# Batch 0 of an attention and SwiGLU kernel: v through the loading queue of q and k, cast on the compute engines

## The chip, the cores and the metric

The kernel runs on one core of one Trainium2 chip. The metric is the device time of one execution in microseconds (us). The kernel before takes 317.82 us, the median of three runs (317.57 to 317.85). One further execution was recorded by the hardware profiler: it took 317.75 us, and the span from its first to its last recorded instruction is 316.0 us. All times inside the kernel below count from the start of that span.

A core has five instruction streams that run side by side and meet at semaphores. TensorE (PE) multiplies matrices, and its weight loads are listed apart as PEld. VectorE (DVE) and ScalarE (ACT) work on elements, GpSimd (POOL) casts and issues DMAs, SyncE (SP) issues DMAs. Each stream executes its instructions strictly in the order in which the program holds them. Sixteen DMA engines move the data that the queues of SP, POOL and ACT ask for.

## The reference

```python
q_s = np.exp(q - np.max(q, axis=-1, keepdims=True))
q_s = q_s / (np.sum(q_s, axis=-1, keepdims=True) + 1e-09)
k_s = np.exp(k - np.max(k, axis=2, keepdims=True))
k_s = k_s / (np.sum(k_s, axis=2, keepdims=True) + 1e-09)
kv = np.einsum('bhsd,bhse->bhde', k_s, v)
attn = np.einsum('bhsd,bhde->bhse', q_s, kv)        # batch 8, heads 8, 576 tokens, head size 64
x = attn.transpose(0, 2, 1, 3).reshape(4608, 512)
g = x @ w_gate                                      # 512 x 1536
out = (g / (1 + np.exp(-g)) * (x @ w_val)) @ w_out  # 1536 x 512
```

This is linear attention: q is normalized over the head dimension, k over the tokens, and the 64x64 product of k and v per head is applied to q. Its output, 4608 tokens of 512 channels, goes through a SwiGLU block. All inputs and the output are float32.

## The kernel before

**Layout.** A batch has 8 heads, handled as two groups G of 4 heads. A loaded tile of q, k or v has 128 partitions: two heads g in the upper and lower half, 64 token blocks each, and along the free axis two heads h and 576 values (9 tokens t of 64). `head_ap` (L65) describes that access to memory, and `load` (L72) issues it on SP into one of three rotating buffers per tensor. A load is 576 KB in float32, in rows of 2304 bytes.

**Attention.** For each group, ScalarE takes the exponent of q and k into bf16 (`exp_of`, L119). VectorE sums q over the head dimension, takes the reciprocal and multiplies (`norm_sum`, `norm_mul`). For batch 0 TensorE transposes the normalized q (`turn_pe`) and a copy moves the result out of PSUM (`turn_out`). `key_sum` (L393) sums the keys by matmuls against the selector `sel`. `kv_first` (L404) multiplies keys by v in 18 matmuls, `scale_first` (L417) divides by the key sums, `x_mm` (L213) applies the result to the transposed q, and `x_out` (L228) copies it to `xt`, which holds x transposed: 4 blocks of 128 channels, blocks 0 and 1 from group 0, blocks 2 and 3 from group 1.

**SwiGLU.** `m_unit` (L286) computes one block m of 128 of the 1536 hidden channels for a chunk of tokens. It contracts `xt` with `wg` into gate banks and with `wv` into value banks, over the 4 channel blocks kk. For 576 tokens it has two parts, of 320 and 256. ScalarE applies Silu, VectorE multiplies into `hr`. `o_mm` (L318) contracts `hr` with `wo`. Twelve units for batch 0 come first, then batch 1's attention among output matmuls, and then eight chunks whose units have the attention of later batches between them.

**What sets the order.** The program is written under a manual schedule: each engine gets its instructions in the order of the source text. Around the change there are these queues:

- SP issues q and k of group 0, then q and k of group 1. The loads of batch 1 follow, and the first of them waits until the second slice of `wo` has landed (L454, `w_dma[-3]`).
- POOL issues v of batch 0 with a cast to bf16 during the transfer (L358 to L361), directly into the constant tiles `v16`; the first of these waits until k of group 0 has landed. Behind them stand the weights, also cast in transfer, in slices of 256, 384, 384 and 512 columns of `wg` and `wv` (L380), then four slices of `wo`. POOL allows eight of its DMAs in flight.
- The text from L426 to L452 sets the order on PE, ACT and DVE: warm-up matmuls (`spin`), key sums, transposes, the kv products, and the copies to `xt`.

In the first unit of batch 0 (`by_part=True`) the steps are sorted by part: gate and value of the first 320 tokens, then of the other 256. [...]

Of the kernel before, what the change touches and what calls it, by code (L numbers as in the profile page):

```python
# [11 lines left out]
SYNC = mybir.DependencyInfo(mybir.DependencyClass.Sync, mybir.DependencyReason.DATA)  # L12
# [3 lines left out]
def kernel(  # L16
# [10 lines left out]
    nc = tc.nc  # L27
# [6 lines left out]
    T = S // 64  # L34
# [27 lines left out]

    raw = {}

    def head_ap(src, b, G, t0=0, t1=T):  # L65
        return bass.AP(
            tensor=src.tensor,
            offset=src[b, 4 * G].offset + 64 * t0,
            ap=[[T * 64, 128], [2 * HSTR, 2], [1, (t1 - t0) * 64]],
        )  # L70

    def load(what, src, b, G, pieces=((0, T),), after=None):  # L72
        t_ = ld.tile([128, 2, T * 64], FP32, tag=what, name=what)
        raw[what, b, G] = t_
        last = None
        for t0, t1 in pieces:
            last = nc.sync.dma_start(out=t_[:, :, 64 * t0:64 * t1], in_=head_ap(src, b, G, t0, t1))
# [54 lines left out]
    def norm_sum(b, G, pieces=((0, T),)):  # L132
        s = st[b, G]
        eq2 = s["eq"].rearrange("p t h d -> p (t h) d")
        rs = at.tile([128, 2 * T], FP32, tag="rs", name="rs")
        first = None
        for t0, t1 in pieces:
            i = nc.vector.reduce_sum(  # L138
                out=rs[:, 2 * t0:2 * t1], in_=eq2[:, 2 * t0:2 * t1, :], axis=mybir.AxisListType.X
            )  # L140
            first = first or i
        rr = s["rr"] = at.tile([128, 2 * T], FP32, tag="rr", name="rr")
        nc.vector.reciprocal(out=rr, in_=rs)
        return first

    def norm_mul(b, G, pieces=((0, T),), engs=None):
# [3 lines left out]
        for (t0, t1), eng in zip(pieces, engs or (nc.vector, nc.vector)):  # L150
            n = 2 * (t1 - t0)
            eng.tensor_mul(  # L152
                qs[:, t0:t1, :].rearrange("p t (h d) -> p (t h) d", d=64),
                eq2[:, 2 * t0:2 * t1, :],
                s["rr"][:, 2 * t0:2 * t1].to_broadcast([128, n, 64]),
            )

    def turn_pe(b, G, i):
        s = st[b, G]
        if i == 0:  # L160
            s["qt"] = at.tile([128, T, 128], BF16, tag="qt", name="qt")
        t0, t1 = BANKS[i]
        tp = s["tp", i] = psp.tile([128, 1024], BF16, tag="ps", name="tp")
        for t in range(t0, t1):
            j = t - t0
            nc.tensor.transpose(  # L166
                out=tp[:, j * 128:(j + 1) * 128], in_=s["qs"][:, t, :], identity=ident
            )
# [15 lines left out]
    def ek_of(b, G, g, t):  # L184
        return st[b, G]["ek"][64 * g:64 * g + 64, t, :, :].rearrange("p h d -> p (h d)")
# [49 lines left out]
    def x_one(b, G):  # L235
        for i in range(2):
            x_out(b, G, i, x_mm(b, G, i))
# [45 lines left out]

    def m_unit(c0, n, m, by_part=False):  # L286
        ms = slice(m * 128, (m + 1) * 128)
        parts = [(c0, n)] if n <= 512 else [(c0, 320), (c0 + 320, n - 320)]
        gu = []
        for nm in ("g_ps", "u_ps"):  # L290
            ps = [bank(nm) for _ in parts]
            gu.append(ps)
        steps = [(a, kk, i) for a in range(2) for kk in range(KT) for i in range(len(parts))]
        if by_part:
            steps.sort(key=lambda a: (a[2], a[0], a[1]))
        for a, kk, i in steps:
            c, w_ = parts[i]
            nc.tensor.matmul(  # L298
                out=gu[a][i][:, 0:w_], lhsT=(wg, wv)[a][:, kk, ms], rhs=xt[:, kk, c:c + w_],
                start=(kk == 0), stop=(kk == KT - 1),  # L300
            )
# [49 lines left out]

    make_identity(nc, ident)
    with tc.manual_schedule():
        kd = []
        for G in range(NG):
            load("q", q, 0, G)
            kd.append(load("k", k, 0, G))
        d = nc.gpsimd.dma_start(out=v16[0], in_=head_ap(v, 0, 0))  # L358
        tc.add_manual_dep(d.ins, kd[0].ins.name, SYNC, reason="order of loads")
        for t0, t1 in BANKS:  # L360
            nc.gpsimd.dma_start(out=v16[1][:, :, 64 * t0:64 * t1], in_=head_ap(v, 0, 1, t0, t1))  # L361

        warm = const.tile([128, 1], FP32, name="warm", tag="warm")
        nc.vector.memset(warm, 0.0)
# [11 lines left out]
        first = norm_sum(0, 0, BANKS)  # L376
        norm_mul(0, 0, BANKS)
        norm_sum(0, 1, BANKS)

        for c0, n in ((0, 256), (256, 384), (640, 384), (1024, 512)):  # L380
            w_slice(wg, moe_w_gate, c0, n)
            w_slice(wv, moe_w_val, c0, n)
        w_dma = [wo_slice(m0, 3) for m0 in (0, 3, 6, 9)]

        def spin(n, after=None):
            idle = bank("idle")
            for _ in range(n):
# [16 lines left out]
        def kv_first(G, t0=0, t1=T):  # L404
            s = st[0, G]
            if t0 == 0:
                s["kv"] = [bank("kv") for _ in range(2)]
            for t in range(t0, t1):
                for g in range(2):
                    r = slice(64 * g, 64 * g + 64)  # L410
                    nc.tensor.matmul(
                        out=s["kv"][g][:, 0:128].rearrange("p (h d) -> p h d", d=64),
                        lhsT=ek_of(0, G, g, t), rhs=v16[G][r, :, 64 * t:64 * t + 64],
                        start=(t == 0), stop=(t == T - 1),
                    )

        def scale_first(G, eng1):  # L417
# [3 lines left out]
            if eng1 is nc.scalar:  # L421
                nc.scalar.mul(kn[:, 1, :], s["kv"][1][:, 0:128], s["kvr"][:, 1:2])
            else:
                nc.vector.tensor_scalar_mul(kn[:, 1, :], s["kv"][1][:, 0:128], s["kvr"][:, 1:2])
# [21 lines left out]
        x_out(0, 0, 0, xp0[0], (nc.scalar, nc.scalar))  # L446
        x_out(0, 0, 1, xp0[1], (nc.vector, None))
        scale_first(1, nc.vector)
        xp1 = x_mm(0, 1, 0), x_mm(0, 1, 1)
        x_out(0, 1, 0, xp1[0], (nc.scalar, nc.vector))  # L450
        x_out(0, 0, 1, xp0[1], (None, nc.vector))
        x_out(0, 1, 1, xp1[1], (nc.scalar, nc.vector))  # L452

        load_batch(1, w_dma[-3], by_group=True)  # L454
        load_batch(2)

        for m in range(MT):
            m_unit(0, S, m, by_part=(m == 0))

        exp_of("q", 1, 0)  # L460
        exp_of("k", 1, 0)
# [121 lines left out]
```

The softmax here doesn't subtract the row's maximum and nothing guards it: scores larger than these inputs give would overflow.

## Time and profile before

| What | Value |
|---|---|
| Median of three runs | 317.82 us |
| Profiled span | 316.0 us |
| PE busy | 304.7 us, 96% |
| DVE busy | 163.2 us, 52% |
| ACT busy | 147.6 us, 47% |
| POOL busy | 28.0 us, 9% |
| SP's queue (q1) | 39.99 MB |
| POOL's queue (q0) | 5.31 MB, counted as written in bf16 |

A table of windows gives, for each stretch of time, its length and then the busy time and the number of instructions of PE, PEld, DVE, ACT and POOL, the granted clock of PE, the share of DMA time and GB/s. A timeline line gives start and duration in us, the engine, the source line, the operation, what it writes from what with its shape, and in brackets how long the engine had been idle before it and what ended the idle time. A line with x2 is two instructions merged. In the rows of DMA queues the columns are packets, MB and the packet time as a share of 16 engines. An idle engine costs time only where it is on the chain that ends last.

### The profile page before, as it was taken

Reading aid. Unit: us, or ns where it says so; the run is one execution under the profiler, and the core shown is the slowest. Engines: PE = TensorE matmul, PEld = TensorE weight load, DVE = VectorE, ACT = ScalarE, POOL = GpSimd, SP = SyncE. Lnnn points to the kernel's source line nnn. Section 1 sums busy time; section 2 is a strip of 40 time slices with the busy share of each in tenths; the row PEclk is TensorE's granted clock in tenths of the full one; section 3 lists DMA queues with packets and bytes.
Section 4 is the critical chain, followed back from the end, with each engine's and each line's share of the span. In section 5 each row is a group of like instructions: output and inputs, shape, how many; then the busy total and the mean of one; then the engine's idle time right before and its main releaser. Section 6 shows DMA issues by size and latency. Waiting matters only on the chain.

```text
span 316.0 us, 4856 instructions
## 1 busy us (share of the span) xinstructions
PE 304.7 (96%) x1865; PEld 152.0 (48%) x1894; DVE 163.2 (52%) x277; ACT 147.6 (47%) x218; POOL 28.0 (9%) x35
## 2 busy tenths in 40 slices
PE   6799999999999999999999999999999999999994
PEld 2477744554444444544454444544454444444443
DVE  3834476685754566455835492639354333423421
ACT  4743488634663465447354637355743113312300
POOL 2930021100200020002000200020000000000000
PEclk9999999999999999999999999999999999999999
DMA  7999999269246806490629253944310202020124
GB/s 269 183 204 207 296 393 391 68 160 364 50 91 179 338 17 128 112 394 11 141 68 352 97 110 66 322 162 103 66 41 0 65 3 66 0 68 3 31 68 102
DMA packets 39304, 45.75 MB, mean 145 GB/s; under 512 B 16368, under 2 KB 23024, under 8 KB 39280
## 3 DMA queue, kind: packets, MB, share of 16 engines
q1 hardware_dynamic: 32480, 39.99, 42.0%
q0 software_dynamic: 6640, 5.31, 10.9%
q8 instruction: 15, 0.25, 0.3%
q10 hardware_dynamic: 160, 0.13, 0.2%
q14 instruction: 9, 0.07, 0.1%
HBM read 37.75 MB, written 9.44 MB: 149 GB/s over the span
## 4 chain that ended last, share of the span: by engine, by line
PE 88%; DMA 4%; DVE 3%; ACT 2%; issue 1%; POOL 1%; SPq 0%; DVEq 0%
PE g_ps L298 29%; PE u_ps L298 29%; PE o_ps L322 25%; PE kv L191 3%; DMA wv<-in_moe_w_val_dram 2%; DMA k<-in_k_dram 2%; DVE rs L138 1%; PE xp L267 1%; DVE qs L152 1%; PE o_ps L342 1%; ACT L124 1%; ACT eq L124 1%; POOL v L361 0%; PE tp L166 0%; POOL v L358 0%
## 5 line engine op out<-in xcount | busy, mean ns | idle before, releaser
L305 ACT ACTIVATE sg<-g_ps 128x512 bf16<-128x512 f32 (+2 forms) x120 | 65.1, 554 | 139.1 <-PE g_ps L298 120.7
L306 DVE TENSOR_TENSOR hr<-sg,u_ps 128x512 bf16<-128x512 bf16 (+2 forms) x120 | 74.5, 630 | 87.8 <-PE u_ps L298 80.4
L298 PE MATMUL g_ps<-xt,wg 128*128 128x512 bf16 (+2 forms) x469 | 110.0, 358 | 1.0 <-ACT xt L111 0.2
L298 PE MATMUL u_ps<-xt,wv 128*128 128x512 bf16 (+2 forms) x468 | 109.8, 357 | 1.2 <-DMA wv<-in_moe_w_val_dram 0.5
L322 PE MATMUL o_ps<-wo,hr 128*128 128x512 bf16 x414 | 93.0, 379 | 0.4 <-issue 0.2
L298 PEld LDWEIGHTS <-wv 128*128 128x128 bf16 x480 | 46.9, 98 | 47.2 <-DMA wv<-in_moe_w_val_dram 0.9
L298 PEld LDWEIGHTS <-wg 128*128 128x128 bf16 x480 | 45.8, 98 | 45.3 <-issue 0.7
L322 PEld LDWEIGHTS <-hr 128*128 128x128 bf16 x420 | 40.9, 98 | 49.1
L113 DVE COPY o_sb<-o_ps 128x512 f32<-128x512 f32 x33 | 22.4, 680 | 39.2 <-PE o_ps L322 37.3
L127 POOL CAST vb<-v 128x1152 bf16<-128x1152 f32 x14 | 16.0, 1146 | 174.3 <-DMA v<-in_v_dram 111.8
L138 DVE TENSOR_REDUCE rs<-eq 128x18 f32<-128x1152 bf16 (+2 forms) x18 | 21.7, 1214 | 13.2 <-ACT eq L124 13.2
L152 DVE TENSOR_TENSOR qs<-eq,rr 128x1152 bf16<-128x1152 bf16 (+2 forms) x18 | 22.1, 1237 | 0.1
L124 ACT ACTIVATE eq<-q 128x1152 bf16<-128x1152 f32 (+2 forms) x18 | 18.1, 1050 | 4.5 <-DMA q<-in_q_dram 4.4
L124 ACT ACTIVATE ek<-k 128x1152 bf16<-128x1152 f32 x16 | 18.0, 1158 | 0.3 <-DMA k<-in_k_dram 0.2
L305 ACT ACT_TABLE_LOAD x12 | 15.4, 1283 | 0.2
L124 ACT ACT_TABLE_LOAD x11 | 14.1, 1283 | 0.2
L388 PE MATMUL idle<-zero 128*128 128x512 bf16 x20 | 6.1, 459 | 3.0 <-DVE rs L138 1.8
L191 PE MATMUL kv<-vb,ek 64*128 64x129 bf16 x252 | 8.7, 217 | 0.0
L191 PEld LDWEIGHTS <-ek 64*128 64x128 bf16 x252 | 7.3, 94 | 2.7 <-ACT sg L305 2.1
L275 ACT CAST xt<-xp 128x512 bf16<-128x512 f32 x12 | 6.4, 588 | 3.6 <-PE xp L267 3.6
L276 DVE CAST xt<-xp 128x512 bf16<-128x512 f32 x12 | 7.7, 683 | 0.0
L347 ACT COPY o_sb<-o_ps 128x128 f32<-128x128 f32 x2 | 0.5, 265 | 13.3 <-DVE o_sb L346 13.3
(46 smaller groups left out, 70.2 us busy)
## 6 DMA issues: line engine op xcount, KB each, us to landing
q<-in_q_dram SPq DMA_DIRECT2D x16, 576.0 KB, 5.6
k<-in_k_dram SPq DMA_DIRECT2D x16, 576.0 KB, 7.3
out_dram<-o_sb SPq DMA_DIRECT2D x70, 128.0 KB, 2.3
v<-in_v_dram SPq DMA_DIRECT2D x14, 576.0 KB, 9.0
wo<-in_moe_w_out_dram POOLq DMA_DIRECT2D x4, 384.0 KB, 16.3
wg<-in_moe_w_gate_dram POOLq DMA_DIRECT2D x2, 384.0 KB, 9.7
wv<-in_moe_w_val_dram POOLq DMA_DIRECT2D x2, 384.0 KB, 10.7
wg<-in_moe_w_gate_dram POOLq DMA_DIRECT2D x1, 512.0 KB, 13.7
```

The lines of the kernel that those rows point to most:

```text
L113: eng.tensor_copy(out=out, in_=in_)
L124: nc.scalar.activation(out=e[:, t0:t1], in_=src[:, t0:t1], func=AF.Exp)
L127: nc.gpsimd.tensor_copy(out=vbs[G][:, :, 0:128].rearrange("p t (h d) -> p t h d", d=64), in_=raw["v", b, G].rearrange("p h (t d) -> p t h ...
L138: i = nc.vector.reduce_sum(out=rs[:, 2 * t0:2 * t1], in_=eq2[:, 2 * t0:2 * t1, :], axis=mybir.AxisListType.X)
L152: eng.tensor_mul(qs[:, t0:t1, :].rearrange("p t (h d) -> p (t h) d", d=64), eq2[:, 2 * t0:2 * t1, :], s["rr"][:, 2 * t0:2 * t1].to_broadca ...
L191: nc.tensor.matmul(out=kv[g][:, c:c + 129], lhsT=ek_of(b, G, g, t), rhs=vbs[G][r, t, 0:129], start=(t == 0), stop=(t == T - 1),)
L275: nc.scalar.copy(out=xt[:, 2 * G, c0:c0 + 512], in_=main[G][0])
L276: nc.vector.tensor_copy(out=xt[:, 2 * G + 1, c0:c0 + 512], in_=main[G][1])
L298: nc.tensor.matmul(out=gu[a][i][:, 0:w_], lhsT=(wg, wv)[a][:, kk, ms], rhs=xt[:, kk, c:c + w_], start=(kk == 0), stop=(kk == KT - 1),)
L305: nc.scalar.activation(out=sg[:, 0:w_], in_=g_ps[:, 0:w_], func=AF.Silu)
L306: nc.vector.tensor_mul(hr[:, m, r:r + w_], sg[:, 0:w_], u_ps[:, 0:w_])
L322: nc.tensor.matmul(out=o_ps, lhsT=hr[:, m, r0:r0 + 128], rhs=wo[:, m, :], start=(m == 0), stop=(m == MT - 1),)
```

## The change

In batch 0, v is no longer loaded by POOL with a cast in transfer. SP's queue now carries, in this order, q and k of group 0, q of group 1, v of group 0, k of group 1, and v of group 1 in two pieces, one for each h. All are whole rows in float32. `load` and `head_ap` select heads instead of token ranges.

The cast is done by compute engines. POOL casts all of v of group 0, ahead of its weight DMAs in its order. For group 1, `cast_half` casts one h at a time, 384 of 576 columns on DVE and 192 on ACT, and `kv_first(1, ...)` works on one h at a time.

The weights come in slices of 128, 128, 256, 512 and 512 columns. The order of `key_sum`, transposes, copies and products on PE, ACT and DVE is rearranged. The copies to `xt` of batch 0 all take one pair of engines, ACT for h=0 and DVE for h=1. In the first unit the steps are sorted by the pair of channel blocks first: gate and value of both parts over blocks 0 and 1 (group 0), then over blocks 2 and 3 (group 1).

```diff
-        kd = []
-        for G in range(NG):
-            load("q", q, 0, G)
-            kd.append(load("k", k, 0, G))
-        d = nc.gpsimd.dma_start(out=v16[0], in_=head_ap(v, 0, 0))
-        tc.add_manual_dep(d.ins, kd[0].ins.name, SYNC, reason="order of loads")
-        for t0, t1 in BANKS:
-            nc.gpsimd.dma_start(out=v16[1][:, :, 64 * t0:64 * t1], in_=head_ap(v, 0, 1, t0, t1))
+        load("q", q, 0, 0)
+        load("k", k, 0, 0)
+        load("q", q, 0, 1)
+        load("v", v, 0, 0)
+        load("k", k, 0, 1)
+        load("v", v, 0, 1, by_head=True)
...
+        nc.gpsimd.tensor_copy(out=v16[0], in_=raw["v", 0, 0])
-        for c0, n in ((0, 256), (256, 384), (640, 384), (1024, 512)):
+        for c0, n in ((0, 128), (128, 128), (256, 256), (512, 512), (1024, 512)):
...
+        def cast_half(h):
+            n = 64 * 6
+            nc.vector.tensor_copy(out=v16[1][:, h, 0:n], in_=raw["v", 0, 1][:, h, 0:n])
+            nc.scalar.copy(out=v16[1][:, h, n:], in_=raw["v", 0, 1][:, h, n:])
...
         spin(6, first)
+        turn_pe(0, 0, 0)
         key_sum(0)
-        turn_pe(0, 0, 0)
         turn_pe(0, 0, 1)
         turn_out(0, 0, 0, nc.scalar)
+        turn_out(0, 0, 1, nc.scalar)
         exp_of("k", 0, 1)
-        turn_out(0, 0, 1, nc.scalar)
         norm_mul(0, 1, BANKS)
         spin(6)
-        key_sum(1)
         kv_first(0)
-        scale_first(0, nc.scalar)
         turn_pe(0, 1, 0)
+        scale_first(0)
         turn_pe(0, 1, 1)
         turn_out(0, 1, 0, nc.vector)
+        key_sum(1)
+        cast_half(0)
+        xp0 = x_mm(0, 0, 0), x_mm(0, 0, 1)
         turn_out(0, 1, 1, nc.vector)
-        xp0 = x_mm(0, 0, 0), x_mm(0, 0, 1)
-        kv_first(1, *BANKS[0])
-        kv_first(1, *BANKS[1])
...
-        scale_first(1, nc.vector)
...
+        kv_first(1, 0, 1)
+        x_out(0, 0, 0, xp0[0])
+        cast_half(1)
+        kv_first(1, 1, 2)
+        scale_first(1)
+        x_out(0, 0, 1, xp0[1])
+        x_one(0, 1)
...
-        if by_part:
-            steps.sort(key=lambda a: (a[2], a[0], a[1]))
+        if first:
+            steps.sort(key=lambda a: (a[1] // 2, a[2], a[0], a[1]))
```

More of the change, by code (lines that the diff above doesn't have):

```diff
@@ L63, with head_ap, load @@
     raw = {}
-    def head_ap(src, b, G, t0=0, t1=T):
+    def head_ap(src, b, G, h=(0, 2)):
         return bass.AP(
             tensor=src.tensor,
-            offset=src[b, 4 * G].offset + 64 * t0,
-            ap=[[T * 64, 128], [2 * HSTR, 2], [1, (t1 - t0) * 64]],
+            offset=src[b, 4 * G + 2 * h[0]].offset,
+            ap=[[T * 64, 128], [2 * HSTR, h[1] - h[0]], [1, T * 64]],
         )
-    def load(what, src, b, G, pieces=((0, T),), after=None):
+    def load(what, src, b, G, after=None, by_head=False):
         t_ = ld.tile([128, 2, T * 64], FP32, tag=what, name=what)
@@ L75, in load @@
         last = None
-        for t0, t1 in pieces:
-            last = nc.sync.dma_start(out=t_[:, :, 64 * t0:64 * t1], in_=head_ap(src, b, G, t0, t1))
+        for h in ((0, 1), (1, 2)) if by_head else ((0, 2),):
+            last = nc.sync.dma_start(out=t_[:, h[0]:h[1], :], in_=head_ap(src, b, G, h))
             if after is not None:
@@ L144, in norm_sum, with norm_mul @@
         return first
-    def norm_mul(b, G, pieces=((0, T),), engs=None):
+    def norm_mul(b, G, pieces=((0, T),)):
         s = st[b, G]
@@ L149, in norm_mul @@
         qs = s["qs"] = at.tile([128, T, 128], BF16, tag="qs", name="qs")
-        for (t0, t1), eng in zip(pieces, engs or (nc.vector, nc.vector)):
+        for t0, t1 in pieces:
             n = 2 * (t1 - t0)
-            eng.tensor_mul(
+            nc.vector.tensor_mul(
                 qs[:, t0:t1, :].rearrange("p t (h d) -> p (t h) d", d=64),
@@ L282, in x_both, with m_unit @@
             )
-    def m_unit(c0, n, m, by_part=False):
+    def m_unit(c0, n, m, first=False):
         ms = slice(m * 128, (m + 1) * 128)
@@ L402, in key_sum, with kv_first @@
             nc.vector.reciprocal(out=s["kvr"], in_=ks[:, 0:2])
-        def kv_first(G, t0=0, t1=T):
+        def kv_first(G, h0=0, h1=2):
             s = st[0, G]
-            if t0 == 0:
+            if h0 == 0:
                 s["kv"] = [bank("kv") for _ in range(2)]
-            for t in range(t0, t1):
+            for t in range(T):
                 for g in range(2):
@@ L411, in kv_first, with scale_first @@
                     nc.tensor.matmul(
-                        out=s["kv"][g][:, 0:128].rearrange("p (h d) -> p h d", d=64),
-                        lhsT=ek_of(0, G, g, t), rhs=v16[G][r, :, 64 * t:64 * t + 64],
+                        out=s["kv"][g][:, 64 * h0:64 * h1].rearrange("p (h d) -> p h d", d=64),
+                        lhsT=ek_of(0, G, g, t), rhs=v16[G][r, h0:h1, 64 * t:64 * t + 64],
                         start=(t == 0), stop=(t == T - 1),
                     )
-        def scale_first(G, eng1):
+        def cast_half(h):
+            n = 64 * 6
+            nc.vector.tensor_copy(out=v16[1][:, h, 0:n], in_=raw["v", 0, 1][:, h, 0:n])
+            nc.scalar.copy(out=v16[1][:, h, n:], in_=raw["v", 0, 1][:, h, n:])
+        def scale_first(G):
             s = st[0, G]
@@ L420, in scale_first @@
             nc.scalar.mul(kn[:, 0, :], s["kv"][0][:, 0:128], s["kvr"][:, 0:1])
[L421 to L424, printed above, removed]
+            nc.vector.tensor_scalar_mul(kn[:, 1, :], s["kv"][1][:, 0:128], s["kvr"][:, 1:2])
         spin(8)
         spin(6, first)
+        turn_pe(0, 0, 0)
         key_sum(0)
-        turn_pe(0, 0, 0)
         turn_pe(0, 0, 1)
         turn_out(0, 0, 0, nc.scalar)
+        turn_out(0, 0, 1, nc.scalar)
         exp_of("k", 0, 1)
-        turn_out(0, 0, 1, nc.scalar)
         norm_mul(0, 1, BANKS)
         spin(6)
-        key_sum(1)
         kv_first(0)
-        scale_first(0, nc.scalar)
         turn_pe(0, 1, 0)
+        scale_first(0)
         turn_pe(0, 1, 1)
         turn_out(0, 1, 0, nc.vector)
+        key_sum(1)
+        cast_half(0)
+        xp0 = x_mm(0, 0, 0), x_mm(0, 0, 1)
         turn_out(0, 1, 1, nc.vector)
-        xp0 = x_mm(0, 0, 0), x_mm(0, 0, 1)
-        kv_first(1, *BANKS[0])
-        kv_first(1, *BANKS[1])
-        x_out(0, 0, 0, xp0[0], (nc.scalar, nc.scalar))
-        x_out(0, 0, 1, xp0[1], (nc.vector, None))
-        scale_first(1, nc.vector)
[L449 to L452, printed above, removed]
+        kv_first(1, 0, 1)
[5 more added lines that the diff above has]
+        x_one(0, 1)
         load_batch(1, w_dma[-3], by_group=True)
@@ L457 @@
         for m in range(MT):
-            m_unit(0, S, m, by_part=(m == 0))
+            m_unit(0, S, m, first=(m == 0))
         exp_of("q", 1, 0)
```

## The prediction

> **What bounds the kernel now.** I read the table of windows first, because it separates the start from the stream: matmuls keep TensorE (PE) busy 21.56 of the 21.56 us from 17.63 to 39.19, and over 99% of the time up to 300 us. Any lasting gain or loss of this change must therefore appear as the moment at which the stream starts.
>
> ```profile
> 0.00:14.87 14.87, 10.30 (x108) 5.18 (x108) 8.49 (x24) 9.14 (x16) 8.93 (x17) 1.00 0.97 228
> 14.87:17.63 2.76, 2.21 (x17) 1.50 (x17) 1.47 (x4) 2.54 (x5) 1.52 (x2) 1.00 1.33 203
> 17.63:39.19 21.56, 21.56 (x179) 17.21 (x176) 8.80 (x22) 8.13 (x24) 1.54 (x2) 1.00 1.23 235
> 39.19:54.14 14.95, 14.31 (x119) 6.99 (x120) 10.90 (x21) 12.28 (x18) 2.28 (x2) 1.00 1.05 392
> ```
>
> Second comes the timeline of the start. The first unit's gate matmuls begin at 14.87; then PE waits for the first slice of `wv`, which ends the wait at 16.2. Unit 1 begins at 17.63, my reference point. On VectorE (DVE), `qs` ends at 12.12, and later waits are short.
>
> ```profile
> 10.69 1.43 DVE L152 TENSOR_TENSOR qs<-eq,rr 128x640 bf16<-128x640 bf16 x2
> 12.53 0.82 DVE L113 COPY qt<-tp 128x640 bf16<-128x640 bf16 x2 [0.34 <-PE tp L166]
> 14.38 0.45 PE L220 MATMUL xp<-qt,kn 64*64 64x320 bf16 x8 [0.44 <-DVE kn L424]
> 14.87 0.79 PE L298 MATMUL g_ps<-xt,wg 128*128 128x320 bf16 x4
> 16.20 0.72 PE L298 MATMUL u_ps<-xt,wv 128*128 128x320 bf16 x4 [0.54 <-DMA wv<-in_moe_w_val_dram]
> 24.49 1.15 PE L298 MATMUL u_ps<-xt,wv 128*128 128x320 bf16 x8
> ```
>
> So weights set the start of the stream, and attention was ready slightly before: the last `xt` copies end near 15.9.
>
> Third, the DMA view cut into windows. Each window's line gives packets, MB and busy share of a queue. From 6 to 8 us only the SyncE queue moves data; the software queue (POOL's) starts after 8, though its first DMA was issued at 6.36, so 1.9 us pass from issue to data. From 13 to 15 its packets write mostly 512 bytes (a 256-column slice in bf16), from 24 to 30 they write 1024.
>
> ```profile
> q1 hardware_dynamic: 354, 0.78, 100.3%
> q0 software_dynamic: 252, 0.27, 86.0%
> DMA packets 751, 0.38 MB, mean 188 GB/s; under 512 B 22, under 2 KB 751, under 8 KB 751
> DMA packets 1244, 1.23 MB, mean 206 GB/s; under 512 B 39, under 2 KB 1244, under 8 KB 1244
> ```
>
> Without the small completion writes that is 729 packets in 2 us on 16 engines, 44 ns each, and 1205 in 6 us, 80 ns each: 36 ns for 512 more bytes. A DMA of 512 descriptors (32 per engine) hence takes 1.4 us at 512 bytes and 2.55 us at 1024.
>
> [...]
>
> **The change part by part.** *Loads.* v leaves POOL's queue and stands fourth and last in SyncE's. The fourth load of that queue landed at 9.57 before (k of group 1: issued 2.27, 7.3 to landing), so v of group 0 lands near 9.6. At the 389 GB/s of the window from 6 to 8 a load of 0.59 MB takes 1.5 us: k of group 1 lands near 11.1 (before 9.57), the two head halves of v near 11.85 and 12.6, where the last v piece before was issued at 7.93 and took 5.6, so landed 13.5. The three added SyncE issues cost some 0.5 us each and end near 4 us, ahead of their data: nothing.
>
> *Cast of v, group 0, on POOL.* A 128x1152 cast costs 1.15 us (the later casts at L127): 9.6 to 10.75. PE's kv matmuls of group 0 can start there instead of at 11.43, which nobody needs yet. But POOL works in order, and behind this cast stand all weight issues. The first goes at 10.75 instead of 8.63, data from 12.65 (1.9 us later), just when the v loads finish, so DMA loses little time.
>
> *Slices.* 256, 384, 384, 512 columns become 128, 128, 256, 512, 512. POOL's two more issues of 0.77 us stay ahead of the data. The 128-column slices write 256-byte packets, 4 DMAs of 32 per engine. The straight line through 44 and 80 ns gives 26 ns each; twice that, 52, is my upper bound, and 44, no cheaper than a 512-byte packet, lies between. I take 26. Then the eighth weight DMA (`wv` to column 1024) ends at 12.65 + 4x0.83 + 2x1.4 + 2x2.55 = 23.9. Unit 4's value matmuls need it; they ran at 24.49 before and will not run before 24.5. The `wv` slices of units 0 to 3 end at 14.3, 16.0 and 18.8, all early. So at 26 ns weights no longer gate anything, and the 16.2 wait goes. The point at which they gate again is 35 ns: 12.65 + 7.9 + 128F = 25.0.
>
> *DVE's queue.* This is what gates instead. From 12.05 DVE runs, in order: scale of kn (0.35), qt copy (0.49), a reciprocal (0.14) behind the key sums, v cast half 0, qt copy (0.42), xt copy (0.49), v cast half 1. Back-to-back starts overlap about 0.08 each (two qt copies: 0.82, not 0.91). The key sums of group 1 now follow the second transposes on PE and end about 12.75, as the exponent of k ends at 11.1+1.16 = 12.26; so the first cast starts near 12.9. [...] Then: cast end 13.1 to 13.3, qt 13.5 to 13.7, xt 13.9 to 14.1, second cast 14.15 to 14.5. Its v half (12.6) has long landed. PE's 18 kv matmuls of the second half: 0.7 (before 0.68 and 0.75), to 14.9 to 15.25. Scale 0.36, to 15.25 to 15.6. From the x matmuls to the first unit 0.5 (14.38 to 14.87), so the unit starts at 15.8 to 16.1.
>
> *ScalarE* has the smaller casts (192 columns, about 0.3 each by the 0.27 of its 128x128 copy), with time before its scale at 15: hidden. Its exponent of k, 1.2 us later, pushes the scale of group 0 to 12.6, before the key sums leave PE free: hidden.
>
> *First unit, group 0 first.* Its first half contracts channels of group 0 (8 matmuls, 0.98), during which ScalarE and DVE copy group 1's xt out (ready 16.2 to 17.1, needed 16.8 to 17.6). So the unit runs unbroken, 1.96 us, and unit 1 starts at 17.75 to 18.1, 0.1 to 0.5 us after 17.63. The Silu table load moves to about 17; the product of unit 0 then ends near 19.3, before its banks are wanted at 19.9: nothing.
>
> [...] POOL issues weights from 10.75 to about 17, each 0.77 us. [...] I take 0.3 for both together, because the trace shows DVE's other copies beside POOL's issues at ordinary lengths.
>
> *Sum.* 0.3 + 0.3 = +0.6 us on the profiled span of 316.0, all passed to the end since PE is full afterwards. ScalarE's chain of batch 1 at 39 moves along. Its loads wait for the second `wo` slice, landed 33.27 before; now 23.9 + 2x2.55 + 2x1.9 = 32.8, not later. The untraced runs were 317.57 to 317.85, about 1.8 above the span, so 317.82 + 0.6 = 318.4.
>
> **Rivals.** (1) *Small packets are slow.* 256-byte packets at 44 ns put the eighth weight DMA at 26.1, unit 4 waits 1.6 after 24.5: 319.4. At 52 ns, 27.2, 2.7: 320.5. For it: [...] software packets between 10.5 and 13 us ran slower than 44 ns in this trace (626 in 2.5 us, 64 ns). Against: 44 and 80 ns lie on a line with little fixed part. It decides from 35 ns on. (2) *Faster.* The attention path ends early and the removed `wv` wait is real gain. The landing of the third load was 2.1 us after the second while others are 1.5 apart; without that lag DVE's sums start up to 0.38 sooner (its wait there). [...] only a start of the first unit before 15.0, 0.8 under my lower end, passes the bound: about 317.0. Against: DVE's list above is a plain sum. [...]
>
> **How the numbers follow.** Main case 0.55, from 317.9 to 318.9 with 318.4 as its centre; small packets 0.22; blocked casts 0.07; faster or early attention 0.16. The measurement can tell about 0.2% (0.64 us) from no change: 318.46 and 317.18 are the borders. The main case gives slower 0.22 and same 0.33; rivals 1 and 3 give slower 0.29; rival 2 same 0.02, faster 0.14. Together faster 0.14, same 0.35, slower 0.51. The range from 317.2 to 320.3 leaves a tenth on each side.
>
> **What would show it.** Right: the first weight issue near 10.7, first unit near 16 without a wait for weights, DVE without a gap from 10.7 to 14.3, unit 1 near 17.9, no later wait of PE for `wv`. Packets that write 256 bytes at 26 ns show rival 1 wrong. The prediction is wrong if PE waits for weights at units 1 to 4, if a DVE cast lasts or waits near 0.8 us, or if unit 1 starts before 17.2.

## The result, and the profile after

The changed kernel takes 319.74 us, the median of four runs (319.43 to 320.31), beside 317.75 us for the kernel before in the same session (317.57 to 317.85, four runs). The ratio is 1.0065, with a 95% interval of 1.0048 to 1.0083: about 2 us slower. The profiled execution took 320.31 us with a span of 318.5 us, 2.5 us more than the 316.0 us of before.

First two windows of the kernel after, the same stretches as before (length; then busy time and instructions of PE, PEld, DVE, ACT and POOL; granted clock; DMA share; GB/s):

```profile
14.87:17.63 2.76, 2.33 (x24) 1.72 (x25) 1.50 (x4) 2.57 (x5) 2.76 (x5) 1.00 1.44 147
17.63:39.19 21.56, 19.25 (x155) 14.72 (x154) 8.28 (x20) 7.17 (x21) 3.75 (x6) 1.00 1.22 204
```

In the second row PE was busy for all of the 21.56 us before; now it is busy for 19.25, so 2.3 us are lost after the stream has started. The waits of PE after 16 us (total, number of times, longest, in us) name what it waited for:

```profile
PE u_ps L298 <- DMA wv<-in_moe_w_val_dram: 1.2, 2, 1.0
PE g_ps L298 <- DMA wg<-in_moe_w_gate_dram: 1.1, 1, 1.1
```

The timeline of the kernel after shows where, and also the steps that the prediction worked out (start, duration, engine, line, operation; idle time and what ended it in brackets). The last line is from SyncE's queue, the first load of batch 1.

```profile
9.73 1.14 POOL L377 CAST v<-v 128x1152 bf16<-128x1152 f32 x1 [8.42 <-DMA v<-in_v_dram]
10.81 0.90 POOL L99 DMA_DIRECT2D wg<-in_moe_w_gate_dram  x1
...
12.94 0.44 DVE L418 CAST v<-v 128x384 bf16<-128x384 f32 x1
14.03 0.34 DVE L418 CAST v<-v 128x384 bf16<-128x384 f32 x1
15.30 0.45 PE L220 MATMUL xp<-qt,kn 64*64 64x320 bf16 x8 [0.44 <-ACT kn L424]
15.68 0.45 PE L298 MATMUL g_ps<-xt,wg 128*128 128x320 bf16 x2
...
17.65 1.14 PE L298 MATMUL g_ps<-xt,wg 128*128 128x320 bf16 x8
20.92 1.15 PE L298 MATMUL g_ps<-xt,wg 128*128 128x320 bf16 x8 [1.14 <-DMA wg<-in_moe_w_gate_dram]
22.29 1.15 PE L298 MATMUL u_ps<-xt,wv 128*128 128x320 bf16 x8 [0.21 <-DMA wv<-in_moe_w_val_dram]
27.34 1.15 PE L298 MATMUL u_ps<-xt,wv 128*128 128x320 bf16 x8 [0.96 <-DMA wv<-in_moe_w_val_dram]
28.33 1.14 PE L298 MATMUL g_ps<-xt,wg 128*128 128x320 bf16 x8
36.22 0.38 SPq L77 DMA_DIRECT2D q<-in_q_dram  x1
```

Unit 1 starts at 17.65, where it started before (17.63). So attention, casts and rearranged first unit cost nothing in this execution. The loss comes after that: unit 2 waits 1.14 us for its gate weights and 0.21 for its value weights, and unit 4 waits 0.96 for its value weights. Unit 5 starts at 28.33. The first load of batch 1, which waits until the second slice of `wo` has landed, is issued at 36.22. The same two in the kernel before:

```profile
25.47 1.14 PE L298 MATMUL g_ps<-xt,wg 128*128 128x320 bf16 x8
...
33.27 0.37 SPq L77 DMA_DIRECT2D q<-in_q_dram  x1
```

From unit 1 to unit 5 the kernel after loses 2.84 us by the starts of the units. That is more than the 2.31 us in brackets, which count from the modelled end of the last matmul: back to back the halves of a unit start 0.98 us apart, though each of them shows 1.14. The whole queue of weights runs 3 us late.

The DMA view of the kernel after tells how the queue got late. These are the sums of three windows: 11.5 to 12.5, 13 to 15 and 17 to 19 us.

```profile
DMA packets 27, 0.02 MB, mean 20 GB/s; under 512 B 20, under 2 KB 20, under 8 KB 27
...
DMA packets 1112, 0.28 MB, mean 139 GB/s; under 512 B 1112, under 2 KB 1112, under 8 KB 1112
...
DMA packets 570, 0.28 MB, mean 141 GB/s; under 512 B 23, under 2 KB 570, under 8 KB 570
```

SyncE's loads are nearly all drained by 11.5 us (its queue fills 31% of the engines from 11.25 to 11.5 and 8% in the next quarter), and the first weight data comes at 12.4, 1.6 us after its issue. Between the two the DMA engines stand almost still (20 GB/s). After that the software queue writes some 140 GB/s until 19 us. Before, it wrote 130 GB/s from 10.5 to 13, and 188 from 13 to 15.

### The profile page after: what moved, and what is told of

Same layout as the page of the kernel before. It is cut to its first block, busy times and chain, and to the rows that moved or that the text cites. A ratio compares the mean times of both kernels' runs of the same rounds, so it can differ in the third digit from the quotient of the medians.

```text
span 318.5 us, 4931 instructions
## 1 busy us (share of the span) xinstructions
PE 306.9 (96%) x1912; PEld 152.0 (48%) x1912; DVE 163.9 (51%) x280; ACT 147.7 (46%) x219; POOL 28.4 (9%) x35
## 4 chain that ended last, share of the span: by engine, by line
PE 88%; DMA 6%; POOL 2%; ACT 1%; DVE 1%; SPq 0%; issue 0%
PE g_ps L298 28%; PE u_ps L298 28%; PE o_ps L322 27%; DMA wv<-in_moe_w_val_dram 4%; PE kv L191 3%; DMA v<-in_v_dram 2%; PE xp L267 1%; POOL wg L99 1%; PE o_ps L342 1%; POOL wv L99 1%; SPq L77 0%; DVE qs L152 0%; DVE rs L138 0%; PE tp L166 0%; ACT L124 0%; ACT eq L124 0%
## 5 line engine op out<-in xcount | busy, mean ns | idle before, releaser
L298 PE MATMUL g_ps<-xt,wg 128*128 128x512 bf16 (+2 forms) x480 | 111.8, 358 | 1.3 <-DMA wg<-in_moe_w_gate_dram 1.1
L298 PE MATMUL u_ps<-xt,wv 128*128 128x512 bf16 (+2 forms) x480 | 111.5, 358 | 1.2 <-DMA wv<-in_moe_w_val_dram 1.2
L127 POOL CAST vb<-v 128x1152 bf16<-128x1152 f32 x14 | 16.1, 1148 | 175.2 <-DMA v<-in_v_dram 174.9
## 6 DMA issues: line engine op xcount, KB each, us to landing
wg<-in_moe_w_gate_dram POOLq DMA_DIRECT2D x2, 512.0 KB, 11.2
```

Source lines behind the costliest of these rows:

```text
L127: nc.gpsimd.tensor_copy(out=vbs[G][:, :, 0:128].rearrange("p t (h d) -> p t h d", d=64), in_=raw["v", b, G].rearrange("p h (t d) -> p t h ...
L298: nc.tensor.matmul(out=gu[a][i][:, 0:w_], lhsT=(wg, wv)[a][:, kk, ms], rhs=xt[:, kk, c:c + w_], start=(kk == 0), stop=(kk == KT - 1),)
```

## Experiments

Four theories were put to the test. **S**: the narrow slices are slow by themselves. **L**: the weights are late, because POOL issues none of them before v has landed and is cast. **C**: TensorE's clock is still at half rate when attention needs it. **C2**: the clock falls back to half rate when attention leaves PE idle. Two readings of each trace carry the argument, so here they are for the kernels that are compared below. All times are in us; the span is that of one profiled execution.

| Kernel | median (kernel before in the same session) | unit 1 starts | batch 1's first load | span | span less that load |
|---|---|---|---|---|---|
| before | 317.75 | 17.63 | 33.27 | 316.0 | 282.7 |
| before, new slices | 317.93 (317.40) | 17.50 | 33.43 | 315.9 | 282.5 |
| before, longer warm-up | 317.54 (317.49) | 17.58 | 33.87 | 316.4 | 282.5 |
| after | 319.74 (317.75) | 17.65 | 36.22 | 318.5 | 282.3 |
| after, old slices | 320.04 (317.40) | 19.11 | 34.40 | 317.1 | 282.7 |
| after, finer late slices | 319.98 (317.40) | 18.11 | 35.84 | 317.9 | 282.1 |
| after, no cast on POOL | 319.58 (317.40) | 18.38 | 34.91 | 317.2 | 282.3 |
| no cast on POOL, warm-up | 319.26 (317.49) | 19.00 | 35.96 | 318.0 | 282.0 |
| after, longer warm-up | 320.08 (317.49) | 17.12 | 35.76 | 318.2 | 282.4 |
| after, warm-up and filling | 319.94 (317.59) | 18.03 | 35.92 | 318.0 | 282.1 |
| weights issued early, warm-up | 320.40 (317.49) | 17.29 | 32.74 | 315.3 | 282.6 |
| weights issued early, filling | 317.87 (317.59) | 17.51 | 32.74 | 315.5 | 282.8 |
| first pair before the cast | 318.14 (317.59) | 17.69 | 32.50 | 315.7 | 283.2 |
| v of group 0 by POOL again | 318.85 (317.60) | 18.45 | 32.46 | 316.5 | 284.0 |

In the six kernels whose batch 1 is loaded later than 34.9 the last column hardly moves: 282.0 to 282.4, whether unit 1 starts at 17.12 or at 19.00. There the end of the weight queue goes with the end of the kernel, and the start of the stream doesn't.

### The slices: undone, taken alone, and cut finer

```diff
# after, old slices
-        for c0, n in ((0, 128), (128, 128), (256, 256), (512, 512), (1024, 512)):
+        for c0, n in ((0, 256), (256, 384), (640, 384), (1024, 512)):
```

> The changed kernel with the weight slices of the kernel before (256, 384, 384, 512 columns). Theory S (the slices cost the 2 us: 2048 packets of 256 bytes, then a 512-column slice that unit 4 has to wait for): the first value slice lands near 15.9, about where attention is ready anyway, later slices are ahead of PE, so the waits at units 2 and 4 (1.14, 0.21 and 0.96 us in the changed kernel) go and the time is 317.7 to 318.3. Theory L (POOL's weight issues begin 2.2 us later behind the cast, whatever their sizes): waits of PE for weights of about 2 us in sum remain, 319.5.

Measured: 320.04 us (319.31 to 322.12, six runs), ratio 1.0096 [1.0072, 1.0120], so no gain, and more than either theory expected. But the trace of this kernel differs in something that wasn't changed. Its timeline:

```profile
6.55 2.74 PE L387 MATMUL idle<-zero 128*128 128x512 bf16 x6 [1.73 <-DVE rs L138]
10.28 2.59 PE L387 MATMUL idle<-zero 128*128 128x512 bf16 x6
...
17.14 0.45 PE L298 MATMUL g_ps<-xt,wg 128*128 128x320 bf16 x2
...
34.40 0.38 SPq L77 DMA_DIRECT2D q<-in_q_dram  x1
```

The six warm-up matmuls take 2.74 us, and those at 10.28 take 2.59; in the profiled executions of before and after they take 1.47 and 1.46. PE runs at half rate until about 12.5 us here, attention is late, and the first unit starts at 17.14 instead of 15.68. (The column of the granted clock says 1.00 in these windows; the durations say otherwise.) This late start hides whether the slices matter. What the trace does show is that PE waits for no weights, and that batch 1's first load goes at 34.40 instead of 36.22. Its fourth weight DMA, `wv` to column 640, landed at 21.5 (issued 13.14, 8.4 to landing). With unit 1 at 17.65 the value matmuls of unit 2 would come 2.94 later, at 20.6, and wait 0.9 by this estimate, where the kernel after waits 2.3 in all. So this median can't be read as saying that the slices don't matter.

The opposite corner is the kernel before with the new slices:

```diff
# before, new slices
-        for c0, n in ((0, 256), (256, 384), (640, 384), (1024, 512)):
+        for c0, n in ((0, 128), (128, 128), (256, 256), (512, 512), (1024, 512)):
```

> The kernel before with the weight slices of the changed one (128, 128, 256, 512, 512). Theory S: small packets cost as much here; the first unit starts up to 1 us earlier, but units 2 and 4 wait for weights, 318.5 to 319.5. Theory L: POOL starts as early as before, so slices of any size arrive in time and the first one earlier: 317.0 to 317.8.

Measured: 317.93 us (317.64 to 318.73, nine runs), ratio 1.0019 [1.0010, 1.0029]. In its timeline unit 4's value matmuls, which need the eighth weight DMA, start at 24.55, and unit 1 at 17.50:

```profile
17.50 1.14 PE L298 MATMUL g_ps<-xt,wg 128*128 128x320 bf16 x8
...
24.55 1.15 PE L298 MATMUL u_ps<-xt,wv 128*128 128x320 bf16 x8
```

Back to back they would come 7 half units of 0.98 us after unit 1, at 24.36; they are 0.2 late. The new slices alone use up the slack of unit 4 and cost 0.5 us in the median. The four corners, read at batch 1's first load in one profiled execution each, are then: before 33.27, slices alone 33.43, all but the slices 34.40, both 36.22. The slices add 0.16 us where weights are issued early and 1.8 where they are issued late. How far such single readings can be trusted is seen in the table where the weights are the same. The kernel before has 33.27, and 33.87 with a longer warm-up. The kernel after has 36.22, 35.76 with a longer warm-up and 35.92 with filling. So the 0.16 can't be told from nothing, and the 1.8 may be 1.4. S falls as a theory of slow packets. That the slices cost more where weights are late is likely, but rests on one execution with old slices and late weights.

Third, the 512-column slice that unit 4 waits for is cut in two:

```diff
# after, finer late slices
-        for c0, n in ((0, 128), (128, 128), (256, 256), (512, 512), (1024, 512)):
+        for c0, n in ((0, 128), (128, 128), (256, 256), (512, 256), (768, 256), (1024, 512)):
```

> The changed kernel with its fourth slice of 512 columns cut into two of 256 (128, 128, 256, 256, 256, 512). Same packets of 256 bytes as the changed kernel. If the size of the slice that unit 4 waits for matters, the wait at unit 4 (0.96 us) goes and 318.8 results; those at unit 2 (1.35 us) stay. If the DMA queue is simply late by 2 us everywhere, the waits move to other units and the time stays at 319.7.

Measured: 319.98 us (319.27 to 320.13, four runs), ratio 1.0075 [1.0062, 1.0088]. Only a small wait for weights is left at unit 2. The time comes back in another place, which the waits of PE between 36 and 60 us show:

```profile
PE tp L166 <- DVE qs L152: 1.2, 2, 0.8
PE kv L191 <- POOL vb L127: 0.3, 1, 0.3
```

These are the transposes and kv products of batch 1. Its loads are still late (35.84), so PE now waits 1.5 us for batch 1's q and v. Waits for weights and waits for batch 1 are two faces of the same late queue: take one away and the other appears.

### The cast taken off POOL

```diff
# after, no cast on POOL (v of group 0 isn't cast; zeros stand in its place)
+        nc.vector.memset(v16[0], 0.0)
-        nc.gpsimd.tensor_copy(out=v16[0], in_=raw["v", 0, 0])
...
+            d = w_slice(wg, moe_w_gate, c0, n)     # the first waits for the load of v of group 0
```

> The changed kernel without POOL's cast of v of group 0: v16 of group 0 is filled with zeros at the start, so heads 0 to 3 of batch 0 get zeros; the first weight DMA waits for the same load of v instead. Weights are issued about 1.1 us earlier (9.7 instead of 10.8), nothing else moves. Theory L: PE's waits for weights (2.3 us in sum) shrink by 1.1 us, 318.6. Theory S: the small packets and the large slice still bind, but a start that is earlier by 1.1 moves their landing as well, unless the loads of v still hold the DMA engines until 12.4: then the gain is under 0.4 and the time 319.4.

Measured: 319.58 us (319.26 to 320.14, four runs), ratio 1.0069 [1.0056, 1.0082]. The first weight goes at 9.56 instead of 10.81, batch 1's first load at 34.91, and one wait of 0.63 us is left at unit 4, although the stream starts late (18.38, half rate until 10 us as above). L has the sign of this right. But in the median nearly nothing is gained, far less than the 1.1 us that L expected.

### A longer warm-up

To take the half rate out of the comparison, the warm-up matmuls start earlier and are more:

```diff
-        spin(8)
-        spin(6, first)
+        spin(16)
+        spin(2, first)
```

It was added to the kernel before and to the kernel after.

> The kernel before with the same longer warm-up. There the first unit waits for wv until 16.2 whatever the clock was before, so full clock by 8.1 buys nothing: 317.3 to 317.8, no change. If a cold clock cost the kernel before as much as it does the changed one, it would gain 0.5 us or more.

> The changed kernel with a longer warm-up: 16 idle matmuls at the start and 2 behind the first sum, instead of 8 and 6, so that TensorE is busy without a break from 1.2 to about 8 us. Four of the six traces so far granted full clock only after 10 us, and there attention of batch 0 came out 0.5 to 1.5 us later than in the two that had it at 4. Theory C (the changed kernel loses its 2 us because attention now decides the start and the clock is cold in most executions): full clock by 8.1, first unit near 15.7 in each, 317.8 to 318.3. Theory L (weights come late in any case: the DMA engines are dry from 11.3 to 12.7 and POOL's queue starts after that): waits for weights of about 2.3 us as in the profiled changed kernel, 319.4 to 319.8.

Measured: the kernel before with it 317.54 us (316.97 to 319.83, 22 runs), ratio 1.0002 [0.9992, 1.0012]; the kernel after with it 320.08 us (319.43 to 321.14, six runs), ratio 1.0080 [1.0064, 1.0095]. In the timeline of the second full rate is there early (the six warm-up matmuls at 8.89 take 1.46 us), the stream starts 0.53 us sooner than in the kernel after (17.12), and PE then waits for weights:

```profile
21.04 1.15 PE L298 MATMUL u_ps<-xt,wv 128*128 128x320 bf16 x8 [0.52 <-DMA wv<-in_moe_w_val_dram]
26.12 1.15 PE L298 MATMUL u_ps<-xt,wv 128*128 128x320 bf16 x8 [0.99 <-DMA wv<-in_moe_w_val_dram]
```

Beside these it waits 0.9 us in batch 1. A sooner start is not worth anything while weights are late, so C doesn't explain the loss.

Now the warm-up together with earlier weights. In the first kernel POOL's cast is left out as above; in the second, the first weight waits only for q of group 1 instead of v of group 0.

```diff
# weights issued early, warm-up
+        q01 = load("q", q, 0, 1)
...
+                tc.add_manual_dep(d.ins, q01.ins.name, SYNC, reason="order of loads")
```

> The longer warm-up, and POOL's cast of v of group 0 left out (zeros instead, so heads 0 to 3 of batch 0 get zeros); the first weight DMA waits for that load of v and is issued at 9.6, 1.1 us before that of the changed kernel. Theory L: waits for weights shrink by about 1 us against the changed kernel with the same warm-up, 318.4 to 318.8. Theory C: no difference to it, both near 318.

> As the last one, but the first weight DMA waits for q of group 1 instead (landed 8.1 in all traces): issues from 8.2, data from 10, as early as in the kernel before, and the DMA engines never run dry. Theory L: no waits for weights at units 1 to 4; the loads of k and v of group 1 give up some bandwidth, so attention comes 0 to 0.7 us later: 317.4 to 318.2. Theory C, or if POOL's queue is slow by itself: 319 or more.

Measured: 319.26 us (318.98 to 320.09, five runs), ratio 1.0049 [1.0036, 1.0062], and 320.40 us (317.36 to 320.89, eleven runs), ratio 1.0071 [1.0050, 1.0091]. The first is slower than either theory expected. Its weights are issued from 9.97, and those of the kernel after with the same warm-up from 10.28; its batch 1 is loaded no sooner (35.96, and 35.76 there). The second is a surprise. Its profiled execution is the fastest of all profiled ones here (317.36, span 315.3), and the timeline has no wait for weights:

```profile
8.21 0.90 POOL L99 DMA_DIRECT2D wg<-in_moe_w_gate_dram  x1 [6.91 <-DMA q<-in_q_dram]
...
17.29 1.14 PE L298 MATMUL g_ps<-xt,wg 128*128 128x320 bf16 x8
```

The edit between the two kernels is the load for which the first weight waits, and nothing else. In their traces it brings the first weight issue forward by 1.76 us (9.97 to 8.21), and batch 1's first load by 3.22 us (35.96 to 32.74). In the medians this gain is hidden, because the eleven runs follow the granted clock of the run: 317.36 us at 1.0, 318.81 to 319.41 at 0.992 to 0.995, 320.40 to 320.89 at 0.988 and 0.989. None of the slow ones was profiled. What probably happens in them is seen in the trace of the first of the two kernels. Its windows from 12 to 18 us:

```profile
12.00:14.00 2.00, 1.46 (x41) 1.00 (x40) 1.96 (x8) 1.53 (x5) 2.00 (x4) 1.00 1.36 129
14.00:16.00 2.00, 1.23 (x27) 0.65 (x27) 1.19 (x5) 0.89 (x3) 2.00 (x3) 0.72 1.40 129
16.00:18.00 2.00, 2.00 (x9) 1.22 (x8) 0.60 (x2) 1.72 (x3) 2.00 (x4) 0.50 1.26 145
```

The clock falls to 0.72 and then to 0.50, and from 16 to 18 us PE executes 9 matmuls where the kernel after executes 18. Attention leaves PE busy for 1.46 and 1.23 of 2 us here. That share alone doesn't decide: in the kernel after PE was busy for 1.47 us from 12 to 14, and for less in the next stretch, and kept full rate:

```profile
14.00:16.00 2.00, 1.14 (x29) 0.71 (x29) 1.34 (x5) 0.95 (x4) 2.00 (x3) 1.00 1.55 154
```

So the rate was taken back in the one trace though PE was busy for more than half of the time (1.46 and 1.23 of 2 us), and kept in the other with less in the second stretch (1.14). How idle PE has to be isn't shown, nor what decides in which runs of one kernel it happens.

### PE kept busy through attention

If C2 is right, more idle matmuls in the gaps of attention keep the clock up. The filling is the same in both kernels:

```diff
         norm_mul(0, 1, BANKS)
-        spin(6)
+        spin(8)
...
         kv_first(1, 0, 1)
+        spin(3)
...
         kv_first(1, 1, 2)
+        spin(2)
```

The first kernel issues weights early, without the cast, as above. The second is the kernel after with warm-up and filling.

> The kernel with early weights and without POOL's cast (zeros for heads 0 to 3 of batch 0), and idle matmuls in the gaps of batch 0's attention on TensorE: 8 instead of 6 ahead of the kv products, 3 between the two halves of group 1, 2 behind them. Its predecessor without the filling took 317.36 us in the run with a granted clock of 1.0 and up to 320.9 in runs with 0.988. Theory C2 (TensorE falls back to the half clock while attention leaves it idle, and the first units then run at half speed): clock at 0.998 or more in every run, median 317.0 to 317.6. If the lower clock has another cause, runs at 0.988 to 0.995 remain, median above 319.

> The changed kernel with the longer warm-up and the same filling, complete otherwise, weights as late as in the change. Theory L (late weights are what the change costs, the clock only what hides behind that wait): clock full in every run, PE still waits for weights by 1.5 to 2.5 us, 319.3 to 319.8. Theory C2 alone: with the clock held the loss is gone, 317.5 to 318.0.

Measured: 317.87 us (317.34 to 318.56, 13 runs), ratio 1.0009 [1.0001, 1.0017], and 319.94 us (318.93 to 320.78, six runs), ratio 1.0069 [1.0054, 1.0084]. Both lie slightly above what the theory that held had expected (317.0 to 317.6, and 319.3 to 319.8). The granted clock is now 0.997 to 1.0 in every run of both. In the windows of the first, PE is busier than above and the clock stays:

```profile
12.00:14.00 2.00, 1.67 (x41) 1.19 (x42) 1.96 (x7) 1.35 (x5) 2.00 (x4) 1.00 1.79 176
14.00:16.00 2.00, 2.00 (x34) 0.93 (x33) 1.18 (x5) 1.09 (x4) 2.00 (x4) 1.00 1.54 198
```

With the clock held in both, the two differ only in when the weights are issued (8.28 and 10.91) and in the cast behind which they stood, and the two together are worth 2.07 us, the whole loss. In the second kernel PE still waits for the eighth weight DMA:

```profile
26.66 1.15 PE L298 MATMUL u_ps<-xt,wv 128*128 128x320 bf16 x8 [0.99 <-DMA wv<-in_moe_w_val_dram]
```

The first kernel has the new slices too, and no wait. Its DMA windows, from 12 to 14 and from 15 to 17 us, show what the packets cost:

```profile
DMA packets 1413, 0.35 MB, mean 176 GB/s; under 512 B 1411, under 2 KB 1413, under 8 KB 1413
...
DMA packets 750, 0.40 MB, mean 199 GB/s; under 512 B 30, under 2 KB 749, under 8 KB 749
```

On 16 engines 1413 packets in 2 us are 23 ns each for 256 bytes, and about 720 without the 30 small ones are 44 ns each for 512. Small packets are cheap here. In the kernel after, the 512-byte packets took 58 ns from 17 to 19 us (16 engines for 2 us, 547 packets).

### Two complete kernels

If the weights must not stand behind the cast, the first pair of slices can be issued ahead of it, with the old slices, warm-up and filling:

```diff
# first pair before the cast
-        nc.gpsimd.tensor_copy(out=v16[0], in_=raw["v", 0, 0])
...
+            if c0 == 0:
+                tc.add_manual_dep(d.ins, q01.ins.name, SYNC, reason="order of loads")
+                nc.gpsimd.tensor_copy(out=v16[0], in_=raw["v", 0, 0])
```

> A complete kernel: the changed one with warm-up and filling, the weight slices of the kernel before, and its first pair of weight DMAs (256 columns) issued ahead of POOL's cast of v, as soon as q of group 1 has landed; the cast then starts near 9.8 as now. Theory L: no DMA gap at 11 to 12.7, weights in time, the first unit near 15.4, 317.2 to 317.8, level with the kernel before or 0.2 us better. If the order on POOL doesn't matter: 319.5.

Measured: 318.14 us (317.69 to 318.62, 20 runs), ratio 1.0015 [1.0008, 1.0022], a little above the 317.2 to 317.8 expected. Its timeline has no wait for weights; the stream starts as in the kernel after (17.69), and batch 1 is loaded 3.7 us sooner:

```profile
32.50 0.38 SPq L77 DMA_DIRECT2D q<-in_q_dram  x1
```

Most of the loss is gone with the loads, the casts and the order of the change in place, and 0.5 us is left. But the slices are the old ones here, and no kernel with the clock held has the old slices and late weights. How much of the 1.80 us against the kernel after with warm-up and filling is due to the order on POOL, and how much to the slices, isn't shown.

The other kernel leaves v of group 0 in POOL's queue with a cast in transfer, ahead of the weights, as before; only v of group 1 goes through SyncE.

```diff
# v of group 0 by POOL again
-        load("v", v, 0, 0)
+        d = nc.gpsimd.dma_start(out=v16[0], in_=head_ap(v, 0, 0))   # waits for k of group 0
```

> A complete kernel that takes the parts that proved harmless: v of group 0 as in the kernel before (POOL's queue, cast in transfer, gated on k of group 0, no cast instruction on POOL), v of group 1 as in the changed one (SyncE, float32, cast by head), slices of the kernel before, order, warm-up and filling as in the last complete kernel but with 2 instead of 3 idle matmuls between the halves. Weights are issued from about 7.2, ahead of their data. Theory L with the clock held: no wait for weights, first unit near 15.3 and unit 1 near 17.3, 317.2 to 317.7, at best 0.3 us better than before. If v on the software queue beside the other loads delays attention, first unit after 16, 318.2 or more.

Measured: 318.85 us (318.76 to 320.99, seven runs), ratio 1.0056 [1.0033, 1.0078], as the second of the two expectations has it. Weights are early (32.46), but v of group 0 shares the engines with SyncE's loads and lands at 12.1, 5.7 us after its issue, so PE waits for it:

```profile
12.19 0.68 PE L410 MATMUL kv<-v,ek 64*128 64x128 bf16 x18 [1.37 <-DMA v<-in_v_dram]
```

Unit 1 then starts at 18.45. The late weights have been traded for a late attention. No kernel tried beats the one before.

## Why the prediction was right or wrong

The measured 319.74 us lies in the upper part of the range, above the 318.9 at which the main case ends. The main case didn't happen, and PE waited for weights at units 2 and 4, which the prediction had named as a sign of being wrong. That the range holds the number is luck: its upper part was there for packets that are slow because they are small and for blocked casts, and neither was the cause.

**Right: the start.** The first weight issue was worked out for 10.75 and came at 10.81; POOL's cast took 1.14 us (1.15). The DVE list held: casts of 0.44 and 0.34 us (their length in the list was the author's estimate, since the kernel before has no such cast), the second ended at 14.37 (14.15 to 14.5), and the first unit started at 15.68 (15.8 to 16.1). Unit 1 started at 17.65 (17.75 to 18.1). Attention gates the start, as said, and in this execution costs 0.02 us against before, not 0.3. The second 0.3 us of the sum was the author's estimate for casts that last longer beside POOL's issues; the trace of the kernel before shows none. It did not show: in the profiled kernel after, POOL issues weights from 10.81 on without a break, and neither cast is long. In two other kernels one of the two casts took 0.58 and 0.73; why isn't shown.

**Wrong: the weights.** The sum for the eighth weight DMA, 23.9, was too small by 3.4: it landed at 27.3 (issued 16.12, 11.2 to landing). Its starting point held, since data came at 12.4 and the sum begins at 12.65. What failed is the price of the packets. The term for the four DMAs of 256-byte packets (3.3 us from 12.65) took 5.1, to 17.8; the two 512-byte DMAs (2.8) took 4.5, to 22.3; the two of 1024 bytes (5.1) took 5.1. The prices of 44 and 80 ns were read in the kernel before where the queue ran at 188 and 206 GB/s, and the 26 was drawn from them; in the kernel after it ran at some 140 GB/s until 19 us. The prediction knew such a slow stretch, the 64 ns from 10.5 to 13, but used it only for a rival. And the statement that batch 1's loads would not go later than 32.8 failed by the same 3.4 us (36.22).

Besides, the step "just when the v loads finish, so DMA loses little time" failed. The landings themselves were as worked out: k of group 1 at 11.2, the first half of v at 11.9, the second at about 12.4. But by 11.5 nearly all of the data had moved, and from 11.75 to 12.5 only five packets of SyncE's queue were left. The step took a landing for the time at which the engines become free, and they stood nearly idle for about a microsecond. That unit 4 would need the eighth DMA, and that it was the place to look, was right; that unit 2 would wait for the fifth wasn't foreseen.

**Right number, wrong cause: the first rival.** Small packets at 52 ns were to put the eighth DMA at 27.2 and the time at 320.5; it landed at 27.3. But the rival put the whole excess on the 256-byte packets, and of the 3.4 us by which the sum was too small 1.7 lie in the two DMAs of 512-byte packets. In the kernel after, packets took 29 ns from 13 to 15 us and 34 from 12.65 to 17.77 (2428 packets, 2081 of them small), hardly below the 35 from which this rival was to decide. Where weights are issued early the same packets cost 23 ns, and the same slices in the kernel before cost 0.2%. So it isn't their size that made them slow. These casting loads read 128 columns, 512 bytes in float32, and write 256; where weights are issued early such a packet costs about half a 512-byte one (23 ns and 44). The 52 ns of this rival was the author's upper bound; windows with 256-byte packets alone show 23 and 29. A load that reads shorter rows was not run.

**What was shown, and what wasn't.** That late issue of weights makes the loss is shown: 2.07 us, the cast included, between two kernels with the clock held, and batch 1's loads sooner by 3.22 us in the traces of two kernels that differ in nothing else. That the cast on POOL is the smaller part of it is seen where it was left out and the weights still waited for v: the median is 319.58 instead of 319.74, and with the warm-up 319.26 instead of 320.08. That the slices make it worse is seen in the four corners at batch 1's first load, in one profiled execution each; in the medians it isn't, since the clock disturbed the kernel with the old slices. Why the software queue runs at some 140 GB/s in the kernel after stays open. The issues alone don't explain it: each takes POOL 0.75 us, and even a slice of 128 columns brings 128 KB as written, 175 GB/s. Nor was POOL only just ahead of the data: the 512-byte packets from 17 to 19 us are those of the DMAs issued at 13.90 and 14.66.

## What to carry to other kernels

Before compute is put ahead of DMA issues on the same engine, work out when the queue behind it *ends*, not only when it begins, and what waits on that end: here the last weights release the next batch's loads, and the wait that finer slices removed at unit 4 came back in batch 1. Narrow first slices were cheap where the weights are issued early (0.5 us in the median) and seem dear where they are late (1.4 to 1.8 us at batch 1's first load, in single executions). And when a stage is moved onto the start's critical path, look at what the tensor clock does there in several runs: idle matmuls in the gaps were worth 2.5 us in the median of one kernel here (320.40 to 317.87).

## What the runs showed of the hardware

- The clock: warm-up matmuls of 512 columns ran at half rate until 10 to 12.5 us in four of the profiled executions (six in 2.74 us), and at full rate from the second group of them on in others of much the same order (six in 1.47). Once granted, full rate was taken back in one trace in which PE was busy for 1.46 and 1.23 of 2 us (granted clock 0.72, then 0.50), and kept in another with 1.47 and 1.14. One kernel's runs spread from 317.36 to 320.89 us with it; with idle matmuls in the gaps all 13 runs had a clock of 0.997 or more.
- The software queue: 256-byte packets at 23 ns and 512-byte at 44 where weights were issued early, but 58 for the same 512 bytes in the kernel after. First data follows the first issue by 1.6 us on an idle queue (10.81 to 12.4); issued at 8.21, while SyncE's loads filled the engines, it came only at 11.
- A 384-column cast from float32 to bf16 on DVE took 0.34 to 0.45 us in 20 of the 22 cases in all kernels, and 0.58 and 0.73 in the other two.
